# Converting the first layer's weights in a PSUM bank without GpSimd, with a longer landing time for DMAs in the plan

## Chip, cores and metric

The kernel runs on one core of a Trainium2 chip. The metric is the device time of one execution in microseconds (us). TensorE (PE) multiplies, VectorE (DVE), ScalarE (ACT) and GpSimd (POOL) do elementwise work, and SyncE (SP) issues all DMAs. Each engine has a queue of its own and works through it in order.

## What is computed

Linear attention, then two feed-forward stages. The inputs of the first weights are 64-bit floats, which the kernel has to read from their two 32-bit words.

```python
q_s = softmax(q, axis=-1); k_s = softmax(k, axis=2)          # batch 4, heads 8, seq 576, head_dim 64
x = einsum('bhsd,bhde->bhse', q_s, einsum('bhsd,bhse->bhde', k_s, v))   # -> 2304 x 512
h = x @ w_in                                                 # 512 -> 2048, float64 weights
x = (h * clip(h + 3, 0, 6) / 6) @ w_out                      # 2048 -> 512, float64 weights
p = domain_probs / (domain_probs.sum(-1) + 1e-9)
out = sum(p[:, e] * (max(x @ w1[e], 0) @ w2[e]) for e in range(4))      # 512 -> 1024 -> 512
```

## The kernel before

Every product is made of two or three matmuls of a number split in a high part (rounded to the form that PE takes) and a low part (the rest). A split is therefore two steps: ScalarE writes the high part, and VectorE or GpSimd subtracts it from the number.

**Order.** The program first notes all steps in a list (`add`), with the engines that may do each, its cost, the steps it needs, and the buffers that it takes and gives back. `Plan.order` then goes through a model of time: whenever an engine is free, it takes the ready step with the least key, mostly the due time. The order so found is the order of each engine's queue. In that model `LAND` is the time from the end of a DMA's slot on SP until a step that needs its data can start. Only the order comes from the model; on the chip each queue waits on semaphores.

**Attention.** For each of four batches, `k_part` handles four head pairs (key maxima L449, exponential L451, transposes on PE L430, copies L456 and L342 or L344, products with v L437, scaling by reciprocal L444 and L445) and `q_part` five tiles of queries (L494 to L507: maxima, subtract on Pool, exponential, sums, reciprocal, multiply on Pool, transposes L492). `x_part` multiplies both (L531) and splits the result in a high (L534, ScalarE) and a low part (L538, VectorE). They use six PSUM banks `pa` (2 to 7) in the first batch and two (2 and 3) later.

**First layer.** Its work is cut in 96 blocks: a chunk c of 128 hidden columns (of 16) by a block of 384 tokens (of 6). `PASSES1` sets which chunks go with which tokens, three to six chunks at a time. `h_part` makes a block's first product (L638 to L640, 12 matmuls of 384 columns), clips it (L652, ScalarE), gates it (L655, VectorE) and splits it (L661, ScalarE; the low part on Pool or VectorE). `y_part` makes the second product (L682, 12 matmuls). A first product takes a PSUM bank of kind `ph`: banks 0 and 1 during attention, and 2 and 3 as well when attention is done. The gate gives it back.

**Conversion of the weights.** `w_half` turns one half (128 x 512) of a chunk's weights from 64-bit floats into a high and a low part, 32 halves in all. In its order: load L576; o1 (L586, VectorE) takes the exponent out of the upper word into a buffer `wt`; o2 (L590, ScalarE) rebases it; o3 and o3b (L592, L595, VectorE) put in the sign and leave the mantissa's upper part in the raw buffer; o4 (L598, ScalarE) makes a float of it there; o5 (L601, VectorE) adds the lower word; o6 (L605, here L347) multiplies by the power of two; o7 (L606, ScalarE) writes the high part into a weight tile; o8 (L609, here L347) writes the low part. L347 is the line of a helper that records an elementwise operation, on Pool if there is a choice; o6 and o8 are on Pool in all 32 halves. The weight tiles of chunks 6 to 15 come free when the last block of an earlier chunk is done.

**Second stage.** `w_prepare` makes seven forms of the last stage's weights during the first layer (L831 on ScalarE, then Pool), stores them in DRAM (`vd`) and reuses the tile; later units load them again (L864). Three units of 768 tokens follow (L1094 and L1216; then L973 and L1289 twice).

Of the kernel before, what the change touches and what calls it, by code (L numbers as in the profile page):

```python
# [9 lines left out]
F32 = mybir.dt.float32  # L10
F32R = mybir.dt.float32r
I32 = mybir.dt.int32
U32 = mybir.dt.uint32
AF = mybir.ActivationFunctionType
ALU = mybir.AluOpType
# [5 lines left out]
DM = H * D  # L21
# [45 lines left out]
NW, NG, NT_ = 24, 2, 3  # L67
# [4 lines left out]
NX, NXG = 24, 7  # L72
# [4 lines left out]


HOPS = {"PE": 0.06, "ACT": 0.05, "DVE": 0.05, "Pool": 0.09, "SP": 0.05, "": 0.0}
LAND = 1.9  # L80


class Cost(float):
# [9 lines left out]
def hop(a, b):  # L93
    return LAND if a == "SP" else HOPS[b]


def dve(n):
    return Cost(0.064 + n / 960)
# [6 lines left out]
def dve2(n):  # L105
    return Cost(0.064 + n / 960, 0.08, True)


def act(n):
    return Cost(0.092 + n / 1200, 0.1)  # L110


def actp(n):
    return Cost(0.05 + n / 1200, 0.1)


def pool_(n):
    return Cost(0.16 + 2.1e-3 * n if n < 600 else 3.25e-3 * n, 0.05, True)
# [10 lines left out]
def dma(n):  # L129
    return Cost(n / 400.0, 0.0)  # L130
# [21 lines left out]
class Plan:  # L152
# [12 lines left out]
    def add(self, eng, fn, deps=(), take=None, give=(), key=None, due=None):  # L165
        self.ops.append(Op(eng, fn, deps, take, give, key, due))
        return self.ops[-1]
# [100 lines left out]
def tile_kernel(ctx: ExitStack, tc: tile.TileContext, q, kt, v, w64, w, p, out):  # L268


    nc = tc.nc
# [39 lines left out]
    PS = [ps.tile([P, 512], F32, name=f"ps{i}") for i in range(8)]  # L311
# [7 lines left out]
    def on(o):  # L319
        return nc.gpsimd if o.on == "Pool" else nc.vector  # L320

    plan = Plan()
    for kind, n in (("kt", 4), ("ek", 3), ("v", 3), ("q", 5), ("pa", 6), ("raw", 4),
                    ("wt", 4), ("w", NW), ("ph", 2), ("g", NG), ("t", NT_), ("x", NX - 4),
                    ("raw2", 0), ("wtmp", 0), ("xt", 0), ("wr", 0),
                    ("raw0", 0), ("wtmp0", 0), ("y", 0)):
        plan.places(kind, range(n))
    add = plan.add
    in_turn = {}

# [15 lines left out]
    def tt(o, out, a, b, op):  # L346
        on(o).tensor_tensor(out=out, in0=a, in1=b, op=op)  # L347
# [203 lines left out]
    def half_sub(o, out, x, hi):  # L551
        tt(o, out, x, hi.bitcast(F32), ALU.subtract)
# [8 lines left out]
    w0, w_done, w_place = {}, {}, {}  # L561
# [12 lines left out]
    def w_half(c, i, space):  # L574
        early = c < PASSES1[0][1]
        ld = load("raw", {"SP": dma(512)}, lambda o: nc.sync.dma_start(  # L576
            out=RAW[o.place].bitcast(mybir.dt.int64), in_=w64[c, i]), (),
            ("raw", lambda n: n < 2 or early))

        def word(k, dt):  # L580
            return RAW[ld.place].bitcast(dt).rearrange("p (n t) -> p n t", t=2)[:, :, k]

        def t(dt):
            return WT[o1.place].bitcast(dt)

        o1 = add({"DVE": Cost(0.33, 0.08, True)}, lambda o: nc.vector.tensor_scalar(  # L586
            out=WT[o.place].bitcast(I32), in0=word(1, I32), scalar1=20, scalar2=0x7FF,
            op0=ALU.logical_shift_right, op1=ALU.bitwise_and), [ld],
            ("wt", lambda n: n < 2 or early))
        o2 = add({"ACT": Cost(0.61, 0.1)}, lambda o: nc.scalar.activation(  # L590
            out=t(I32), in_=t(I32), func=AF.Relu, scale=2.0**23, bias=rebase), [o1])
        o3 = add({"DVE": dve2(DM)}, lambda o: nc.vector.scalar_tensor_tensor(  # L592
            out=t(I32), in0=word(1, I32), scalar=-(2**31), in1=t(I32),
            op0=ALU.bitwise_and, op1=ALU.bitwise_or), [o2])
        o3 = add({"DVE": Cost(0.33, 0.08, True)}, lambda o: nc.vector.tensor_scalar(  # L595
            out=word(1, I32), in0=word(1, I32), scalar1=0xFFFFF, scalar2=None,
            op0=ALU.bitwise_and), [o3])
        o4 = add({"ACT": act(DM)}, lambda o: nc.scalar.activation(  # L598
            out=word(1, F32), in_=word(1, I32), func=AF.Copy, scale=2.0**-20, bias=1.0),
            [o3])  # L600
        o5 = add({"DVE": dve2(DM)}, lambda o: nc.vector.scalar_tensor_tensor(  # L601
            out=word(1, F32), in0=word(0, U32), scalar=2.0**-52, in1=word(1, F32),
            op0=ALU.mult, op1=ALU.add), [o4])
        o6 = add({"Pool": pool_(DM), "DVE": dve2(DM)}, lambda o: tt(
            o, t(F32), word(1, F32), t(F32), ALU.mult), [o5], None, [("raw", ld)])  # L605
        o7 = add({"ACT": act(DM)}, lambda o: nc.scalar.activation(  # L606
            out=w0[c, i, 0], in_=t(F32), func=AF.Copy), [o6] + space)
        o8 = add({"Pool": pool_(DM), "DVE": dve2(DM)}, lambda o: half_sub(
            o, w0[c, i, 1], t(F32), w0[c, i, 0]), [o7], None, [("wt", o1)])  # L609
        stage_ops.append(o8)  # L610
        return o8

# [789 lines left out]
    for i in range(RING):  # L1402
        o = add(NONE, lambda o: None, ring, ("w", None), (), 0.0)
        o.give.append(("wr", o))
    for i in range(MORE_W + RING):
        o = add(NONE, lambda o: None, stage2, ("wr", None), (), 0.0)
# [6 lines left out]
    for i in range(NXG):  # L1413
        o = load("xg", NONE, lambda o: None, [evicted[NK - 1]], ("x", None), 0.0)
# [120 lines left out]
```

## Time and profile before

| what | value |
|---|---|
| three runs | 1231.95, 1235.85, 1236.56 us; median 1235.85 |
| profiled execution | 1234.68 us, its span 1232.9 us |
| busy share of the span | PE 97%, VectorE 63%, POOL 61%, ScalarE 49% |
| granted clock of PE, mean | 0.994 of full |

The page gives the busy time of each engine, its course in 40 slices, and the chain of work that ended last. PE is busy 5, 6, 9 and 9 tenths in the first four slices of 31 us each, and 9 or more in nearly all others. Of the other views, the windows give busy time by stretch, the timeline gives single instructions with the idle time ahead of each and what ended it, the groups by line and shape give counts and mean durations, and the list of waits says who waited for whom. A step's duration in these rows reaches a little into that of its successor: an undisturbed step of VectorE on 512 columns lasts 0.68 us, and the next one starts 0.60 us after it.

### The profile page before, as it was taken

The page shows a single profiled execution, that of the slowest core. Times are in us where ns is not written, and L with a number is a line of the kernel's source. Part 1 is how long each engine was busy: PE and PEld are TensorE (multiplying, and loading weights), DVE is VectorE, ACT ScalarE, POOL GpSimd, SP SyncE. Part 2 cuts the span into 40 slices and gives each one's busy share as a digit, 9 for nine tenths or more (in the row PEclk, how much of TensorE's full clock was granted, in tenths as well). Part 3 has the DMA queues.
Part 4 walks back from the last instruction along what each step waited for, and adds up shares of the span by engine and source line. Part 5 has one row for each costly group of instructions (what it writes and reads, how often), then busy time and mean ns, then how long its engine had stood idle before and what let it go on. Part 6 is the DMA issues. An engine that isn't in the chain of part 4 may idle for free.

```text
span 1232.9 us, 21178 instructions
## 1 busy us (share of the span) xinstructions
PE 1197.6 (97%) x7296; PEld 1146.5 (93%) x7296; DVE 779.1 (63%) x1362; ACT 600.7 (49%) x1256; POOL 757.7 (61%) x780
## 2 busy tenths in 40 slices
PE   5699999999999999999999999999999999999998
PEld 4589999999999999988988889999999999999998
DVE  6877731668763555555555575666666966666665
ACT  6667544645554543644444444444444544444441
POOL 4677677766688630877777705655555565555552
PEclk9899999999999999999999999999999999999999
DMA  9533444244367430565555547877777787777771
GB/s 318 154 95 104 162 162 164 103 145 147 135 222 256 152 131 1 178 214 180 182 182 190 183 159 232 275 248 250 249 248 250 241 294 250 247 247 249 246 249 59
DMA packets 125275, 238.99 MB, mean 194 GB/s; under 512 B 14064, under 2 KB 14064, under 8 KB 125168
## 3 DMA queue, kind: packets, MB, share of 16 engines
q1 hardware_dynamic: 125168, 237.64, 57.9%
q8 instruction: 58, 0.95, 0.3%
q14 instruction: 49, 0.40, 0.1%
HBM read 174.14 MB, written 63.44 MB: 193 GB/s over the span
## 4 chain that ended last, share of the span: by engine, by line
PE 80%; POOL 6%; DMA 5%; DVE 4%; issue 3%; ACT 1%; SPq 0%; DVEq 0%; POOLq 0%; ACTq 0%
PE ps L1289 19%; PE ps L973 19%; PE ps L1216 11%; PE ps L1094 9%; PE ps L682 9%; POOL w L347 3%; PE ps L638 3%; PE ps L640 3%; PE ps L639 3%; DMA vd<-w 3%; POOL st L347 1%; DMA qs<-in_q_dram 1%; PE ps L437 1%; POOL wtmp L347 1%; PE ps L531 1%
## 5 line engine op out<-in xcount | busy, mean ns | idle before, releaser
L973 PE MATMUL ps<-x,w 128*128 128x384 f32 x1344 | 264.4, 335 | 0.0
L1289 PE MATMUL ps<-w,g 128*128 128x256 f32 x1737 | 244.0, 283 | 1.7 <-DVE acc L1338 1.7
L347 POOL TENSOR_TENSOR w<-st,w 128x256 fp32r<-128x256 f32 (+1 forms) x174 | 173.8, 1016 | 114.7 <-ACT w L931 76.8
L1289 PEld LDWEIGHTS ps<-w,g 128*128 128x128 f32 x1737 | 228.6, 189 | 5.0 <-DVE acc L1338 5.0
L682 PE MATMUL ps<-g,w 128*128 128x384 f32 x1152 | 223.2, 339 | 5.0 <-ACT g L661 4.1
L973 PEld LDWEIGHTS ps<-x,w 128*128 128x128 f32 x1344 | 227.2, 189 | 0.8
L347 POOL TENSOR_TENSOR g<-t,g 128x384 fp32r<-128x384 f32 x128 | 140.9, 1109 | 124.8 <-ACT g L996 108.4
L682 PEld LDWEIGHTS ps<-g,w 128*128 128x128 f32 x1152 | 199.4, 188 | 12.4 <-ACT g L661 7.6
L1338 DVE SCALAR_TENSOR_TENSOR acc<-ps,pt,acc 128x256 f32<-128x256 f32 x312 | 144.2, 480 | 99.2 <-PE ps L1289 97.6
L1216 PE MATMUL ps<-w,g 128*128 128x512 f32 x576 | 148.9, 394 | 0.0
L1094 PE MATMUL ps<-x,w 128*128 128x384 f32 x672 | 131.0, 335 | 0.0
L655 DVE SCALAR_TENSOR_TENSOR r<-r,ps 128x384 f32<-128x384 f32 x96 | 53.0, 552 | 122.1 <-ACT r L652 114.4
L638 PE MATMUL ps<-x,w 128*128 128x384 f32 x384 | 129.0, 336 | 0.0
L640 PE MATMUL ps<-x,w 128*128 128x384 f32 x384 | 128.5, 335 | 0.3 <-POOL w L347 0.3
L639 PE MATMUL ps<-x,w 128*128 128x384 f32 x384 | 128.3, 334 | 0.0
L1094 PEld LDWEIGHTS ps<-x,w 128*128 128x128 f32 x672 | 119.4, 188 | 7.8
L1216 PEld LDWEIGHTS ps<-w,g 128*128 128x128 f32 x576 | 106.6, 188 | 16.7
L347 POOL TENSOR_TENSOR st<-st 128x256 f32<-128x256 f32 (+1 forms) x66 | 74.4, 1131 | 48.6 <-DVE st L601 45.3
L996 ACT ACTIVATE g<-t 128x384 fp32r<-128x384 f32 x143 | 74.6, 525 | 59.3 <-DVE t L1038 21.6
L652 ACT ACTIVATE r<-ps,three 128x384 f32<-128x384 f32 x96 | 55.4, 577 | 76.1 <-PE ps L640 75.0
L347 POOL TENSOR_TENSOR t<-t 128x384 f32<-128x384 f32 x47 | 47.9, 1020 | 45.3 <-ACT t L981 38.9
L981 ACT ACTIVATE t<-ps 128x384 f32<-128x384 f32 x104 | 50.3, 484 | 52.1 <-PE ps L973 51.5
(145 smaller groups left out, 1852.4 us busy)
## 6 DMA issues: line engine op xcount, KB each, us to landing
w<-wd SPq DMA_DIRECT2D x224, 256.0 KB, 3.1
w<-vd SPq DMA_DIRECT2D x224, 256.0 KB, 3.6
vd<-w SPq DMA_DIRECT2D x112, 256.0 KB, 2.2
wd<-w SPq DMA_DIRECT2D x112, 256.0 KB, 3.5
st<-in_w_dram SPq DMA_DIRECT2D x64, 256.0 KB, 3.5
st<-in_w_dram SPq DMA_DIRECT2D x30, 512.0 KB, 3.9
raw<-in_w_dram SPq DMA_DIRECT2D x32, 256.0 KB, 3.7
out_dram<-acc SPq DMA_DIRECT2D x18, 256.0 KB, 2.5
```

The source lines that it names most:

```text
L347: on(o).tensor_tensor(out=out, in0=a, in1=b, op=op)
L638: nc.tensor.matmul(pst[0], lhsT=hi, rhs=a, start=(k == 0), stop=False)
L639: nc.tensor.matmul(pst[0], lhsT=hi, rhs=b, start=False, stop=False)
L640: nc.tensor.matmul(pst[0], lhsT=lo, rhs=a, start=False, stop=(k == NK - 1))
L652: nc.scalar.activation(out=pst["r"], in_=pst[0], func=AF.Relu, bias=three)
L682: nc.tensor.matmul(y, lhsT=l, rhs=r, start=(s["start"] and not low and m == 0), stop=(s["stop"] and bool(low)))
L973: nc.tensor.matmul(bank(i), lhsT=l, rhs=r, start=(opens and k == 0 and m == 0), stop=(k == 1 and m == 2), skip_group_check=not opens)
L996: nc.scalar.activation(out=made[i][0][:, :n], in_=at(src), func=AF.Relu if raw else AF.Copy)
L1094: nc.tensor.matmul(bank(i), lhsT=l, rhs=r, start=(opens and k == 0 and m == 0), stop=(k == 1 and m == 2), skip_group_check=not opens)
L1216: nc.tensor.matmul(y, lhsT=l, rhs=rr, start=opens and x == 0, stop=closes and x == len(seq) - 1)
L1289: nc.tensor.matmul(y, lhsT=l, rhs=r, start=clears and x == 0, stop=x == len(seq) - 1, skip_group_check=True)
L1338: o1 = add({"DVE": dvep(half)}, lambda o: nc.vector.scalar_tensor_tensor(out=a, in0=y, scalar=s, in1=a, op0=ALU.mult, op1=ALU.add), [made])
```

## The change

`w_half` makes steps o4 to o8 in a PSUM bank. ScalarE's o4 writes the float there, VectorE's o5 and o6 work in it in place, ScalarE's o7 reads it for the high part, and VectorE's o8 reads it for the low part. Pool takes part in none of it. The bank is number 1, a buffer kind `pw` with one place; it is taken by o4 and given back by o8. Kind `ph` loses it: one bank (0) during attention and three (0, 2 and 3) afterwards. The raw buffer is given back by o5 instead of o6, and `wt` by o6 instead of o8. The weight tiles (`space`) are now needed by o4 instead of o7. Apart from that `LAND` is 4.0 instead of 1.9, which reorders all queues. Since lines are added, those behind L598 have numbers higher by 2 to 5 in the changed kernel: the first product is L643 to L645 there, the second L687, the clip L657, the gate L660, the high part of a split L666, a weight form L836, o4 L602, o5 L605, o6 L608, o7 L610 and o8 L612; attention's lines are higher by 1.

```diff
-LAND = 1.9
+LAND = 4.0
...
-                    ("wt", 4), ("w", NW), ("ph", 2), ("g", NG), ("t", NT_), ("x", NX - 4),
+                    ("wt", 4), ("w", NW), ("ph", 1), ("g", NG), ("t", NT_), ("x", NX - 4),
...
+    plan.places("pw", [1])
...
+        def f():
+            return PS[o4.place]
+
         o4 = add({"ACT": act(DM)}, lambda o: nc.scalar.activation(
-            out=word(1, F32), in_=word(1, I32), func=AF.Copy, scale=2.0**-20, bias=1.0),
-            [o3])
-        o5 = add({"DVE": dve2(DM)}, lambda o: nc.vector.scalar_tensor_tensor(
-            out=word(1, F32), in0=word(0, U32), scalar=2.0**-52, in1=word(1, F32),
-            op0=ALU.mult, op1=ALU.add), [o4])
-        o6 = add({"Pool": pool_(DM), "DVE": dve2(DM)}, lambda o: tt(
-            o, t(F32), word(1, F32), t(F32), ALU.mult), [o5], None, [("raw", ld)])
-        o7 = add({"ACT": act(DM)}, lambda o: nc.scalar.activation(
-            out=w0[c, i, 0], in_=t(F32), func=AF.Copy), [o6] + space)
-        o8 = add({"Pool": pool_(DM), "DVE": dve2(DM)}, lambda o: half_sub(
-            o, w0[c, i, 1], t(F32), w0[c, i, 0]), [o7], None, [("wt", o1)])
+            out=f(), in_=word(1, I32), func=AF.Copy, scale=2.0**-20, bias=1.0),
+            [o3] + space, ("pw", None))
+        o5 = add({"DVE": dve(DM)}, lambda o: nc.vector.scalar_tensor_tensor(
+            out=f(), in0=word(0, U32), scalar=2.0**-52, in1=f(),
+            op0=ALU.mult, op1=ALU.add), [o4], None, [("raw", ld)])
+        o6 = add({"DVE": dve(DM)}, lambda o: nc.vector.tensor_tensor(
+            out=f(), in0=f(), in1=t(F32), op=ALU.mult), [o5], None, [("wt", o1)])
+        o7 = add({"ACT": actp(DM)}, lambda o: nc.scalar.activation(
+            out=w0[c, i, 0], in_=f(), func=AF.Copy), [o6])
+        o8 = add({"DVE": dve(DM)}, lambda o: nc.vector.tensor_tensor(
+            out=w0[c, i, 1], in0=f(), in1=w0[c, i, 0].bitcast(F32), op=ALU.subtract),
+            [o7], None, [("pw", o4)])
```

The order moves in all queues. Three places follow, of before and of the changed kernel each. The first is VectorE where the low parts of the third token block's x (x0_20 to x0_23) stand, for which PE waits at 61.20 us. Before:

```order
L601 SCALAR_TENSOR_TENSOR acc_81<-acc_81 128x512
L592 SCALAR_TENSOR_TENSOR acc_81<-acc_81 128x512
L592 SCALAR_TENSOR_TENSOR st0_113<-st0_113 128x512
L595 TENSOR_SCALAR acc_81<-acc_81 128x512
L538 TENSOR_TENSOR x0_20_167<-ps3_118,x0_20_167 128x384
L538 TENSOR_TENSOR x0_21_168<-ps2_117,x0_21_168 128x384
L499 TENSOR_REDUCE qm1_105<-qs1_98 128x8
L494 TENSOR_REDUCE qm3_107<-spare2_111 128x8
L494 TENSOR_REDUCE qm4_108<-spare3_112 64x8
L538 TENSOR_TENSOR x0_22_169<-ps3_118,x0_22_169 128x384
L538 TENSOR_TENSOR x0_23_170<-ps2_117,x0_23_170 128x384
```

Here VectorE in the changed kernel (ps1 is the bank of the conversion):

```order
L612 TENSOR_TENSOR w_1_1_1_157<-ps1_116,w_1_1_0_156 128x512
L450 TENSOR_REDUCE nm1_101<-acc_81 128x1
L450 TENSOR_REDUCE nm2_102<-acc_81 128x1
L605 SCALAR_TENSOR_TENSOR ps1_116<-st0_113,ps1_116 128x512
L450 TENSOR_REDUCE nm3_103<-spare0_109 128x1
L539 TENSOR_TENSOR x0_20_166<-ps3_118,x0_20_166 128x384
L608 TENSOR_TENSOR ps1_116<-ps1_116,st0_113 128x512
L539 TENSOR_TENSOR x0_21_167<-ps2_117,x0_21_167 128x384
L495 TENSOR_REDUCE qm2_106<-qs2_99 128x8
L539 TENSOR_TENSOR x0_22_168<-ps3_118,x0_22_168 128x384
L612 TENSOR_TENSOR w_2_0_1_159<-ps1_116,w_2_0_0_158 128x512
L539 TENSOR_TENSOR x0_23_169<-ps2_117,x0_23_169 128x384
```

Before, four steps of three halves stand ahead of the x steps; now the last four steps of conversions ahead of and among them (o8 of w_1_1, then o5, o6 and o8 of w_2_0) all work in bank 1.

The second place is PE behind the first product of block 0 with chunk 0 (its last matmul, L640 or L645, is the first row). Before, up to the transposes of the next keys:

```order
L640 MATMUL ps0_115<-x0_03_152,w_0_0_1_148 128x384
L492 MATMUL ps3_118<-ident_87,qs0_97 128x128 x4
L492 MATMUL ps2_117<-ident_87,qs1_98 128x128 x4
L531 MATMUL ps3_118<-qt_86,bd2_91 128x192
L531 MATMUL ps2_117<-qt_86,bd0_89 128x192
L437 MATMUL ps3_118<-vs0_95,acc_81 128x129 x5
L531 MATMUL ps2_117<-qt_86,bd3_92 128x192
L531 MATMUL ps3_118<-qt_86,bd2_91 128x192
L437 MATMUL ps2_117<-vs1_96,acc_81 128x129 x5
L531 MATMUL ps3_118<-qt_86,bd1_90 128x192
L531 MATMUL ps2_117<-qt_86,bd3_92 128x192
L492 MATMUL ps3_118<-ident_87,qs2_99 128x128 x4
```

In the changed kernel, up to the second product of the same block:

```order
L645 MATMUL ps0_115<-x0_03_151,w_0_0_1_147 128x384
L532 MATMUL ps2_117<-qt_86,bd3_92 128x192
L438 MATMUL ps3_118<-vs1_96,acc_81 128x129 x5
L532 MATMUL ps2_117<-qt_86,bd0_89 128x192
L532 MATMUL ps3_118<-qt_86,bd3_92 128x192
L532 MATMUL ps2_117<-qt_86,bd1_90 128x192
L532 MATMUL ps3_118<-qt_86,bd2_91 128x192
L431 MATMUL ps2_117<-ident_87,acc_81 128x128 x4
L431 MATMUL ps3_118<-ident_87,acc_81 64x128
L687 MATMUL ps4_119<-g_503,w_0_1_0_152 128x384
```

Before, the second product stands behind fourteen rows of attention work, in the changed kernel behind eight; the first product with chunk 1 follows it there at once, where before nine more rows of attention work stand among and behind the second product's rows.

The third place is ScalarE in the first layer's later passes, near the conversion of chunk 11. Rows L831 or L836 write the forms of the last stage's weights (w_7_5_1 is form 5 of pair 7); a conversion writes w_11_0_0. Before:

```order
L831 ACTIVATE w_7_7_1_2777<-wtmp_2608 128x256
L652 ACTIVATE r_2820<-ps0_115,three_84 128x384
L831 ACTIVATE w_7_5_1_2828<-wtmp_2661 128x256
L661 ACTIVATE g_2834<-r_2820 128x384
L598 ACTIVATE st0_113<-st0_113 128x512
L590 ACTIVATE st1_114<-st1_114,rebase_85 128x512
L831 ACTIVATE w_7_6_1_2860<-wtmp_2685 128x256
L652 ACTIVATE r_2864<-ps1_116,three_84 128x384
L661 ACTIVATE g_2875<-r_2864 128x384
L606 ACTIVATE w_11_0_0_2416<-st0_113 128x512
```

Now:

```order
L602 ACTIVATE ps1_116<-st0_113 128x512
L836 ACTIVATE w_6_7_1_2815<-wtmp_2617 128x256
L657 ACTIVATE r_2819<-ps3_118,three_84 128x384
L610 ACTIVATE w_11_0_0_2359<-ps1_116 128x512
L836 ACTIVATE w_6_5_1_2828<-wtmp_2636 128x256
L666 ACTIVATE g_2837<-r_2819 128x384
L602 ACTIVATE ps1_116<-st1_114 128x512
```

Beside the same conversion stand forms of pair 7 before and of pair 6 now.

## Rows read from the trace of the kernel before

**Rows 1.** The page: span, and busy time of PE (share, instructions).

```profile
span 1232.9 us, 21178 instructions
PE 1197.6 (97%) x7296; PEld 1146.5 (93%) x7296; DVE 779.1 (63%) x1362; ACT 600.7 (49%) x1256; POOL 757.7 (61%) x780
```

**Rows 2.** Windows: length, PE, PEld, DVE, ACT, POOL busy, granted clock, DMA share, GB/s.

```profile
41.98:71.50 29.52, 21.77 (x112) 16.18 (x111) 25.41 (x54) 19.50 (x44) 17.62 (x15) 0.88 0.40 119
71.50:106.80 35.30, 33.79 (x218) 30.75 (x219) 26.74 (x59) 25.56 (x56) 24.29 (x21) 1.00 0.36 113
...
30.00:40.00 10.00, 7.62 (x38) 6.72 (x39) 7.68 (x21) 4.62 (x13) 7.56 (x7) 0.67 0.59 186
60.00:70.00 10.00, 8.80 (x38) 7.15 (x39) 8.01 (x19) 4.32 (x10) 6.83 (x7) 0.66 0.19 46
```

**Rows 3.** Timeline of PE, attention: start, length, line; in brackets idle time and releaser.

```profile
31.29 1.30 PE L430 MATMUL ps<-ident,acc 128*128 128x128 f32 x5 [2.98 <-DVE bd L445]
...
61.20 2.93 PE L531 MATMUL ps<-qt,bd 128*128 128x384 f32 x4 [3.32 <-DVE x L538]
```

**Rows 4.** Timeline of VectorE: gates 1, 2 and 8, and two equal steps.

```profile
41.44 0.54 DVE L655 SCALAR_TENSOR_TENSOR r<-r,ps 128x384 f32<-128x384 f32 x1
...
57.12 0.68 DVE L592 SCALAR_TENSOR_TENSOR acc<-acc 128x512 int32<-128x512 int32 x1
57.72 1.78 DVE L592 SCALAR_TENSOR_TENSOR st<-st 128x512 int32<-128x512 int32 x1
...
71.28 0.55 DVE L655 SCALAR_TENSOR_TENSOR r<-r,ps 128x384 f32<-128x384 f32 x1 [0.47 <-ACT r L652]
...
106.29 0.56 DVE L655 SCALAR_TENSOR_TENSOR r<-r,ps 128x384 f32<-128x384 f32 x1 [0.36 <-ACT r L652]
```

**Rows 5.** Groups, 41.98 to 106.8 us (mean ns); then by line (least/median/most ns).

```profile
L601 DVE SCALAR_TENSOR_TENSOR st<-st 128x512 f32<-128x512 uint32 x5 | 4.7, 934 | 0.0
L592 DVE SCALAR_TENSOR_TENSOR st<-st 128x512 int32<-128x512 int32 x5 | 4.6, 921 | 1.2 <-ACT st L590 1.2
L595 DVE TENSOR_SCALAR st<-st 128x512 int32<-128x512 int32 x6 | 3.6, 603 | 0.0
...
L601 DVE SCALAR_TENSOR_TENSOR st<-st x30: 679/686/1774, 29.4 to 419.8; 128x512 f32<-128x512 uint32 x30
L592 DVE SCALAR_TENSOR_TENSOR st<-st x30: 636/689/1814, 20.8 to 417.4; 128x512 int32<-128x512 int32 x30
L595 DVE TENSOR_SCALAR st<-st x30: 372/421/1424, 21.7 to 418.5; 128x512 int32<-128x512 int32 x30
```

**Rows 6.** Helper line L347: least/median/most ns; last row, o6 in 0 to 110 us.

```profile
L347 DVE TENSOR_TENSOR t<-ps,t x79: 541/558/559, 506.1 to 1211.9; 128x384 f32<-128x384 f32 x79
L347 DVE TENSOR_TENSOR g<-r,g x69: 544/560/1629, 128.3 to 497.9; 128x384 fp32r<-128x384 f32 x69
L347 DVE TENSOR_TENSOR t<-t x26: 546/560/1116, 504.0 to 1166.5; 128x384 f32<-128x384 f32 x26
...
L347 POOL TENSOR_TENSOR st<-st 128x512 f32<-128x512 f32 x7 | 10.1, 1439 | 7.4 <-DVE st L601 7.4
```

**Rows 7.** Waits (total us, times, longest), then timeline rows of ACT, PE and POOL.

```profile
ACT w L831 <- DMA vd<-w: 43.0, 45, 4.1
PE ps L682 <- ACT g L661: 4.1, 7, 1.5
...
290.97 0.42 ACT L831 ACTIVATE w<-wtmp 128x256 fp32r<-128x256 f32 x1 [4.13 <-DMA vd<-w]
291.85 2.35 PE L682 MATMUL ps<-g,w 128*128 128x384 f32 x12 [1.47 <-ACT g L661]
494.31 2.53 POOL L347 TENSOR_TENSOR w<-st,w 128x512 fp32r<-128x512 f32 x2 [51.19 <-ACT w L931]
```

**Rows 8.** DMA issues: count, KB each, median us from issue to landing.

```profile
acc<-in_kt_dram SPq DMA_DIRECT2D x13, 288.0 KB, 3.5
st<-in_w_dram SPq DMA_DIRECT2D x30, 512.0 KB, 3.9
```

## The prediction, made before the changed kernel ran

> **What bounds the kernel now.** I read the page's head and busy times first [rows 1]: TensorE is busy 97% of the span, so a change elsewhere counts only where PE stands still or runs slowly. The windows place this: PE is busy 21.8 of the 29.5 us up to 71.5 us, and 33.8 of the 35.3 behind [rows 2]; after 90 us nearly all of the rest is a few stalls of the first layer's later passes, 4.1 us in seven waits of PE's second products for a split made by ScalarE [rows 7]. So two places can move the end: the attention stage up to about 107 us, and the stretch from 240 to 420 us. Behind them the queues of PE, ScalarE, VectorE and SP hold the same kinds of operation in the same order before and after, and PE never waits for a load there; I cost this part at nothing. What hides it is a full PE; if its loads came late they would show as PE waits on w<-wd.
>
> In the attention stage PE waits for VectorE: at 31.29 us for the scaling of a head pair, at 61.20 us for a low part of x [rows 3]. VectorE's queue shows why [rows 4]: 57.12 and 57.72 us are the same operation of two weight halves, 0.60 us apart when undisturbed, and the second took 1.78. Between the first gate (41.44 us) and the second (71.28 us) VectorE is busy 25.4 of 29.5 us, 86%; from there to the eighth gate (106.29 us) 26.7 of 35.3, 76%, since PE is then the limit [rows 2, 4]. A gate is the VectorE step L655 of a first-layer block, and counts blocks.
>
> **The change, part by part.** *Conversion.* Each of 32 halves moves two Pool operations (o6 and o8; 1.44 us for o6 in the first 110 us [rows 6]) to VectorE, as operations with an operand in PSUM. No row shows VectorE reading and writing one PSUM bank; the bounds are 0.60 us, the start-to-start time of a 512-wide step [rows 4], and 0.93, the mean of such a step under Pool's disturbance [rows 5]. I take 0.60, since steps with a PSUM operand show no disturbance: 541/558/559 ns (least, median, most), against 1629 ns at most for one with all operands in SBUF [rows 6].
>
> [...]
>
> *What VectorE has to do up to the eighth gate.* By then the changed order has as many first products on PE as before, 36 more second-product matmuls (some 6 us) and less attention work of about the same 6 us (three kv groups, ten transposes of k, four 192-wide x products): PE's task up to this gate is equal. VectorE's between gates 1 and 8 is not. Added: 16 operations o6 and o8 (9.6 us), two more o5 and one more o3 (1.8), two key maxima, two evictions and the four steps on the shares that stood ahead of gate 1 before (3.4). Gone: four reciprocal and scaling pairs, two sums, five 192-wide low parts, one o1 (4.9). Sum: 9.9 us more.
>
> Against that stands relief. In this stretch 16 of the port-sharing steps run 934, 921 and 603 ns on average where their medians are 686, 689 and 421: (0.248 x 5) + (0.232 x 5) + (0.182 x 6) = 3.5 us, 0.22 each [rows 5]. There are 29 such steps of four lines before, 6.4 us, and 22 after. Pool's 41.9 us of work in the two windows [rows 2] falls by 14 operations of about 1.4 us to half; I estimate 22 x 0.11 = 2.4 us. Relief: 4.0 us.
>
> So VectorE has 52.1 + 9.9 - 4.0 = 58.0 us to do where it had 52.1 in 64.8. If it is now the limit all the way and keeps the 86% of the first window, that takes 58.0 / 0.861 = 67.4 us, **2.6 us more**. PE cannot win lost time back, since it is full behind. The share is the unknown: 93% gives 62.4 us (-2.4), the second window's 76% gives 76.6 us (+11.8). I take 86%, the row of the stretch in which VectorE is the limit now.
>
> *One bank instead of two for first products (ph), one for the conversion (pw).* With one ph bank a first product waits for the gate of the last. In the changed PE order a second product (12 matmuls, 2.35 us with the last one's tail [rows 7]) or attention work stands between them nearly everywhere; the gate, 0.54 us [rows 4], and a clip of like length on ScalarE come after the product, so this hides unless VectorE's queue is late, which the share above covers. After attention three banks are left of four, with two such products, some 4.2 us, per block: nothing. The PSUM bank is held from o4 to o8, five steps that alternate between ScalarE and VectorE, some 3 us at least if ScalarE's two steps are as long as VectorE's three.
>
> *Space.* o4 now waits for the weight tiles, where only o7 did. Behind o4 on ScalarE stand clips and splits of the main work. This matters once, where chunks 6 to 8 take the tiles of chunks 0 to 2: six halves in about six blocks of 4.2 us. At 4 us each it is just enough; PE would lose under 1 us.
>
> *LAND.* Loads of keys and weights take 3.5 and 3.9 us [rows 8], not 1.9: the plan now counts 4.0. In the first layer's later passes ScalarE stood 43.0 us in 45 waits for a weight form's tile that a store still read; one of them, 4.13 us up to 290.97, delayed the split behind it and so PE at 291.85 by 1.47 [rows 7]. The changed order has these forms some seven places later beside the same conversion. It can return up to the 4.1 us of PE's waits. But VectorE has more there too, since 20 of the halves are converted in it (24 us more) while Pool has less. Ends: -4.1 and +3; I take -1. Pool's forms end about three blocks later; its pause of 51.19 us behind them covers this [rows 7].
>
> **Sum.** Start +2.6, later passes -1, the rest 0: +1.6 us. The profiled execution was 1234.68 us around a span of 1232.9, 1.2 us under the median of 1235.85; its sum is 1236.3, and moved to the median it is **1237.5**.
>
> **Rivals.** *VectorE and ScalarE wait for each other (slower).* A half now hands over four times between two queues that each run in order; Pool, which took two of the five steps, let VectorE go on. In the changed VectorE queue o5, o6 and o8 stand between the x steps on which PE waits; a late o7 on ScalarE stops them all. If the busy share falls to the second window's 76%, the stage is 11.8 us longer and no gain is left later: 1247.7. It decides slower from a share of 81% (58.0 / 0.81 = 71.6, +6.8). For it: two hand-overs more per half, and VectorE's 58 us there are 8 us per block where PE needs some 4.2 and the attention work. Against: ScalarE's own load does not grow. 0.31.
>
> *The order fits the chip (faster).* [...] 0.26.
>
> *The bank is too slow at the turn of the tiles.* At 5.5 us per half the six halves take 8 us more than six blocks: 1244. Part of the slower chance (0.04 of it).
>
> *The change does nothing*, because the attention stage is paced by its loads and buffers: 1235.9, within the forecast's case.
>
> **How the numbers follow.** Forecast 0.43 (own range 1231 to 1243), slower rivals 0.31, faster rival 0.26. No change that a measurement here can tell is within 0.5%, 6.2 us: 1229.7 to 1242.0. The range reaches to both sides' rivals and leaves out about one in ten at each end: 1226 to 1249. Faster 0.26, same 0.43, slower 0.31.
>
> **What would show it.** Right: gate 8 at 107 to 111 us, VectorE busy 85% or more from gate 1 to gate 8, Pool under 25 us there, the port-sharing steps near their medians. Slower rival: idle time of VectorE ahead of o5, o6 and o8, put down to ScalarE. Faster rival: gate 8 before 104 us, no window of low clock, no ScalarE wait for vd<-w over 2 us. Wrong altogether: PE waits behind 500 us, or steps on PSUM of 0.75 us and more.

## The result, and the profile after

The changed kernel took **1213.26 us** (median of four runs, 1212.97 to 1213.55), against 1235.54 for the kernel before: a ratio of 0.9825, 95% interval [0.9805, 0.9845]. That is 22 us less. The prediction was 1237.5 with a range of 1226 to 1249, so it was wrong: next to no change was forecast, and the range ends 13 us above the time.

The head of the page after (span, busy times, the shares of the chain that ended last) stands against [rows 1]:

```profile
span 1210.9 us, 21155 instructions
PE 1190.0 (98%) x7296; PEld 1145.9 (95%) x7296; DVE 790.3 (65%) x1426; ACT 593.0 (49%) x1255; POOL 665.6 (55%) x717
PE 92%; DVE 5%; ACT 1%; issue 0%; POOL 0%; DMA 0%; DVEq 0%; ACTq 0%; POOLq 0%
```

One pair of numbers holds the whole result. The weight loads of PE (PEld) are 7296 in both, and busy 1146.5 us before and 1145.9 after. So the time in which PE loaded no weights is 1232.9 - 1146.5 = 86.4 us before and 1210.9 - 1145.9 = 65.0 after: 21.4 us less, of 22.0 us of span. The matmul row shows two thirds of it: 1232.9 - 1197.6 = 35.3 us not busy before, 20.9 after.

Where it went is read from the gates. The timeline of VectorE after (start, length, line; idle time and releaser in brackets), gates 1, 2, 8, 15, 36 and 78, against [rows 4]:

```profile
38.84 0.55 DVE L660 SCALAR_TENSOR_TENSOR r<-r,ps 128x384 f32<-128x384 f32 x1 [0.32 <-ACT r L657]
52.34 0.54 DVE L660 SCALAR_TENSOR_TENSOR r<-r,ps 128x384 f32<-128x384 f32 x1
94.67 0.54 DVE L660 SCALAR_TENSOR_TENSOR r<-r,ps 128x384 f32<-128x384 f32 x1
137.88 0.55 DVE L660 SCALAR_TENSOR_TENSOR r<-r,ps 128x384 f32<-128x384 f32 x1 [2.46 <-ACT r L657]
225.31 0.56 DVE L660 SCALAR_TENSOR_TENSOR r<-r,ps 128x384 f32<-128x384 f32 x1 [0.40 <-ACT r L657]
400.63 0.55 DVE L660 SCALAR_TENSOR_TENSOR r<-r,ps 128x384 f32<-128x384 f32 x1 [0.83 <-ACT r L657]
```

Gates 15, 36 and 78 of the kernel before, in the same view:

```profile
149.11 0.56 DVE L655 SCALAR_TENSOR_TENSOR r<-r,ps 128x384 f32<-128x384 f32 x1 [1.24 <-ACT r L652]
236.47 0.56 DVE L655 SCALAR_TENSOR_TENSOR r<-r,ps 128x384 f32<-128x384 f32 x1 [3.60 <-ACT r L652]
421.81 0.56 DVE L655 SCALAR_TENSOR_TENSOR r<-r,ps 128x384 f32<-128x384 f32 x1 [1.37 <-ACT r L652]
```

With gate 15 attention is over in both. By then 11.2 us are gained. From gate 15 to 36 both take 87.4 us, from 36 to 78 the changed kernel takes 175.3 instead of 185.3 (10.0 us), and behind gate 78 the two differ by 0.8 us. So there are two gains: 11 us in the attention stage and 10 us in the later passes of the first layer.

The windows of both kernels say what each gain is made of (length; busy time of PE, PEld, DVE, ACT, POOL; granted clock; DMA share; GB/s). Before, up to gate 15 and from gate 36 to 78:

```profile
0.00:149.11 149.11, 125.08 (x725) 109.30 (x726) 113.89 (x242) 99.69 (x215) 95.97 (x92) 0.95 0.51 165
236.47:421.81 185.34, 179.95 (x1010) 173.71 (x1009) 119.66 (x193) 97.97 (x204) 135.97 (x146) 1.00 0.51 174
```

After, up to gate 15, from gate 1 to past the eighth, between gates 15 and 36, and from gate 36 to 78:

```profile
0.00:137.88 137.88, 122.02 (x725) 107.77 (x726) 116.16 (x264) 95.54 (x209) 56.94 (x64) 0.99 0.52 173
38.84:95.23 56.39, 52.87 (x305) 45.46 (x303) 55.60 (x124) 43.08 (x95) 25.01 (x25) 0.97 0.42 136
137.88:225.31 87.43, 87.43 (x507) 87.43 (x506) 29.46 (x52) 38.10 (x83) 48.54 (x60) 1.00 0.35 121
225.31:400.63 175.32, 175.32 (x1009) 174.56 (x1009) 125.66 (x222) 97.98 (x214) 100.36 (x128) 1.00 0.58 198
```

Up to gate 15 PE does the same task, 726 weight loads in both. They are busy 109.30 us before and 107.77 after, 1.5 us less at a granted clock of 0.99 instead of 0.95; and PE stands without a weight load for 39.8 us before and 30.1 after, 9.7 less. In the later passes the weight loads stand still for 11.6 us before and 0.8 after. 21 blocks with full weight loads take 87.4 us, so 42 take 174.8: the changed kernel is at that pace, and the kernel before lost 10.5 us against it.

What the weight loads waited for from 225 to 420 us (total us, times, longest), before:

```profile
PEld ps L682 <- ACT g L661: 7.6, 11, 1.8
PEld ps L682 <- DVE g L347: 1.6, 4, 0.7
PEld ps L682 <- DVE acc L724: 0.7, 4, 0.2
PEld ps L640 <- POOL w L347: 0.7, 1, 0.7
PEld ps L682 <- issue: 0.6, 1, 0.6
```

And after:

```profile
PEld ps L687 <- ACT g L666: 0.6, 2, 0.3
PEld ps L645 <- DVE w L612: 0.2, 1, 0.2
```

11.2 us in 21 waits before, mostly for the split that ScalarE writes, and 0.8 after. ScalarE's own waits for vd<-w, of which [rows 7] shows 43.0 us in the whole run, 33.2 of them from 225 to 420 us, are gone there: no row of that kind is left for ScalarE. The two hang together. Each wait of the weight loads can be followed back in the trace, from what ended it to what that step had waited for itself. Of the 21 waits before, 15 (8.3 of the 11.2 us) lead back so to a wait of ScalarE for a store, some directly, some by way of VectorE or Pool; after, none does.

### The profile page after: what moved, and what is told of

It reads as the page before. It is cut to its first block, busy times and chain, and to the rows that moved or that the text cites. A ratio compares the mean times of both kernels' runs of the same rounds, so it can differ in the third digit from the quotient of the medians.

```text
span 1210.9 us, 21155 instructions
## 1 busy us (share of the span) xinstructions
PE 1190.0 (98%) x7296; PEld 1145.9 (95%) x7296; DVE 790.3 (65%) x1426; ACT 593.0 (49%) x1255; POOL 665.6 (55%) x717
## 4 chain that ended last, share of the span: by engine, by line
PE 92%; DVE 5%; ACT 1%; issue 0%; POOL 0%; DMA 0%; DVEq 0%; ACTq 0%; POOLq 0%
PE ps L1294 19%; PE ps L978 18%; PE ps L687 16%; PE ps L1221 11%; PE ps L1099 10%; PE ps L645 5%; PE ps L643 5%; PE ps L644 5%; PE ps L438 1%; PE ps L532 1%; PE ps L431 1%; DVE acc L1343 1%; DVE x L348 0%; DVE x L539 0%; PE ps L493 0%
## 5 line engine op out<-in xcount | busy, mean ns | idle before, releaser
L978 PEld LDWEIGHTS ps<-x,w 128*128 128x128 f32 x1344 | 227.2, 189 | 0.8
L687 PE MATMUL ps<-g,w 128*128 128x384 f32 x1152 | 223.2, 339 | 1.6 <-ACT w L610 1.2
L348 POOL TENSOR_TENSOR g<-t,g 128x384 fp32r<-128x384 f32 x131 | 144.4, 1113 | 126.5 <-ACT g L1001 111.2
L687 PEld LDWEIGHTS ps<-g,w 128*128 128x128 f32 x1152 | 201.8, 189 | 4.4 <-ACT w L610 1.4
L348 POOL TENSOR_TENSOR w<-st,w 128x256 fp32r<-128x256 f32 (+1 forms) x144 | 133.0, 944 | 106.1 <-ACT w L936 66.6
L660 DVE SCALAR_TENSOR_TENSOR r<-r,ps 128x384 f32<-128x384 f32 x96 | 53.0, 552 | 118.0 <-ACT r L657 114.9
L643 PE MATMUL ps<-x,w 128*128 128x384 f32 x384 | 129.0, 336 | 0.0
L645 PE MATMUL ps<-x,w 128*128 128x384 f32 x384 | 128.6, 335 | 0.3 <-DVE w L612 0.3
L1099 PEld LDWEIGHTS ps<-x,w 128*128 128x128 f32 x672 | 119.4, 188 | 7.8
L657 ACT ACTIVATE r<-ps,three 128x384 f32<-128x384 f32 x96 | 55.7, 581 | 138.6 <-PE ps L645 138.2
L1001 ACT ACTIVATE g<-t 128x384 fp32r<-128x384 f32 x160 | 82.8, 524 | 80.0 <-DVE t L1065 36.7
L348 POOL TENSOR_TENSOR w<-wtmp,w 128x256 fp32r<-128x256 f32 x64 | 49.7, 779 | 50.8 <-ACT w L836 50.7
L645 PEld LDWEIGHTS ps<-x,w 128*128 128x128 f32 x384 | 72.1, 188 | 0.8 <-DVE w L612 0.8
L643 PEld LDWEIGHTS ps<-x,w 128*128 128x128 f32 x384 | 72.1, 188 | 0.2
```

What stands on the lines that cost most here:

```text
L643: nc.tensor.matmul(pst[0], lhsT=hi, rhs=a, start=(k == 0), stop=False)
L645: nc.tensor.matmul(pst[0], lhsT=lo, rhs=a, start=False, stop=(k == NK - 1))
L657: nc.scalar.activation(out=pst["r"], in_=pst[0], func=AF.Relu, bias=three)
L687: nc.tensor.matmul(y, lhsT=l, rhs=r, start=(s["start"] and not low and m == 0), stop=(s["stop"] and bool(low)))
L978: nc.tensor.matmul(bank(i), lhsT=l, rhs=r, start=(opens and k == 0 and m == 0), stop=(k == 1 and m == 2), skip_group_check=not opens)
L1001: nc.scalar.activation(out=made[i][0][:, :n], in_=at(src), func=AF.Relu if raw else AF.Copy)
```

## The experiments

Two parts of the change can be set apart at once: the number `LAND`, and the conversion in PSUM. The table holds what all runs gave; the reading of each stands below it. "Busy" and "still" are the weight loads' time up to gate 15 and the rest of the time up to it (the task is equal: 726 weight loads by that gate in all, but 720 in dve_extra; the busy time goes with the granted clock, from 105.5 us at 1.00 in dve_sbuf to 110.0 at 0.95 in land_only). The last two columns are gate 36 to 78, and the sum of the weight loads' waits from 225 to 420 us. The gates are those of one traced execution of each kernel. Each ratio is to runs of the kernel before made beside that kernel; their median was 1233.1 us for free_4, load_4, pool_junk and dve_extra and 1235.5 to 1235.7 for the others, so small differences between medians of the two groups mean little.

| kernel | median us | ratio to before | gate 15 | busy | still | 36 to 78 | waits |
|---|---|---|---|---|---|---|---|
| before | 1235.5 | | 149.1 | 109.3 | 39.8 | 185.3 | 11.2 |
| changed | 1213.3 | 0.9825 [0.9805, 0.9845] | 137.9 | 107.8 | 30.1 | 175.3 | 0.8 |
| land_only | 1223.2 | 0.9907 [0.9885, 0.9928] | 147.0 | 110.0 | 37.0 | 176.3 | 1.6 |
| psum_only | 1228.1 | 0.9944 [0.9927, 0.9960] | 140.6 | 106.3 | 34.3 | 183.6 | 10.9 |
| dve_sbuf | 1218.2 | 0.9866 [0.9849, 0.9884] | 140.6 | 105.5 | 35.2 | 177.3 | 2.0 |
| pool_junk | 1220.0 | 0.9892 [0.9874, 0.9910] | 141.1 | 107.5 | 33.7 | 178.0 | 3.5 |
| free_4 | 1222.6 | 0.9908 [0.9892, 0.9924] | 141.6 | 108.9 | 32.7 | 179.2 | 4.7 |
| load_4 | 1222.8 | 0.9907 [0.9889, 0.9926] | 138.3 | 108.9 | 29.4 | 184.8 | 12.3 |
| one_bank | 1230.0 | 0.9958 [0.9946, 0.9971] | 149.9 | 109.1 | 40.8 | 177.8 | 3.3 |
| space_late | 1212.5 | 0.9815 [0.9801, 0.9830] | 136.9 | 105.9 | 31.0 | 175.1 | 0 |
| dve_extra | 1222.5 | 0.9908 [0.9892, 0.9924] | 141.1 | 106.5 | 34.6 | 179.6 | 5.0 |
| shares_late | 1214.4 | 0.9832 [0.9817, 0.9847] | 138.1 | 105.9 | 32.2 | 175.4 | 0.8 |
| land3 | 1218.6 | 0.9864 [0.9849, 0.9878] | 144.1 | 109.5 | 34.6 | 174.9 | 0.2 |
| land6 | 1220.6 | 0.9882 [0.9865, 0.9898] | 140.9 | 108.9 | 32.0 | 177.1 | 2.6 |

In twelve of these fourteen kernels the last two columns agree within 1 us when 174.8 is taken from the first of them (185.3 - 174.8 = 10.5 beside 11.2), and in the other two (psum_only and load_4) within 2.4; there 1003 and 999 weight loads lie between the two gates, in the others 1007 to 1011. So the weight loads' waits are the loss.

**One half of the change each.** The kernel before with the longer landing time:

```diff
-LAND = 1.9
+LAND = 4.0
```

> The kernel before with the landing time at 4.0 alone; the conversion stays with Pool in SBUF. Theory 1 (the attention stage gains 11 us by the conversion in PSUM, the later passes 10 us by the landing time): about 1225 us, gate 15 near 149 us as before, gates 36 to 78 in some 175 us instead of 185. Theory 2 (the landing time, and so the order, gives both): 1213 to 1216 us, gate 15 near 138 us. Theory 3 (the conversion gives both): 1233 to 1237 us.

The changed kernel with the old one:

```diff
-LAND = 4.0
+LAND = 1.9
```

> The changed kernel with the landing time back at 1.9. Theory 1: about 1224 us, gate 15 at 138 to 140 us, gates 36 to 78 in some 185 us. Theory 2: 1233 us or more, gate 15 at 149 us or later, since VectorE has more to do and the order is the old one in kind. Theory 3: 1213 to 1216 us.

The landing time alone gives 12.3 us, 9.0 of them in gates 36 to 78 and 2.1 by gate 15. The conversion alone gives 7.4: 8.5 by gate 15, and nothing from there to gate 78, which takes 272.8 us against 272.7 before. 12.3 and 7.4 make 19.7 of the 22: the two gains have different causes in the main. The later passes are the landing time's, as ScalarE's waits from 225 to 420 us show. land_only:

```profile
ACT w L831 <- DMA vd<-w: 1.4, 1, 1.4
```

psum_only:

```profile
ACT w L836 <- DMA vd<-w: 25.9, 28, 2.7
```

With 1.9 in the plan ScalarE still comes 28 times to a tile that a store still reads; with 4.0, on the old conversion, once. The stores themselves say why. A store of 256 KB has a slot of 0.64 us in the plan, so with 1.9 behind it the tile counts as free after 2.5 us, and with 4.0 after 4.6. Of the 74 stores of the kernel before that were issued from 225 to 420 us, 35 took longer than 2.5 us to land and two longer than 4.6; the median was 2.3, the longest 5.7, and that one is behind the wait of 4.13 us in [rows 7].

**Which DMAs the landing time is about.** In the model it counts twice: for a step that needs a load's data, and for a buffer that a DMA has to give back. Each run takes 4.0 for one of them and 1.9 for the other:

```diff
 def hop(a, b):
-    return LAND if a == "SP" else HOPS[b]
+    return (LAND if b else FREE) if a == "SP" else HOPS[b]
```

In free_4 the 4.0 stands for the buffer, in load_4 for the data.

> The changed kernel with the landing time split: 4.0 only where a DMA frees a buffer, 1.9 where a step waits for a load's data. If the later passes are cured because forms no longer stand on ScalarE ahead of the stores that free their tiles: gates 36 to 78 in 175 to 177 us, ScalarE waits for vd<-w under 3 us in 225 to 420 us, and about 1214 to 1218 us. If it is the loads' time: 183 us or more for these gates and 1221 us or more.

> The other half: 4.0 where a step waits for a load's data, 1.9 where a DMA frees a buffer. If the release counts: gates 36 to 78 in 182 us or more, ScalarE waits for vd<-w of 20 us or more, about 1221 to 1226 us. If the loads count: 1213 to 1217 us.

From 225 to 420 us, ScalarE's waits for stores and those of the weight loads, in free_4 (4.0 for what a DMA gives back):

```profile
ACT w L837 <- DMA vd<-w: 0.4, 1, 0.4
PEld ps L688 <- ACT g L667: 2.3, 3, 1.1
PEld ps L688 <- DVE g L349: 1.9, 2, 1.3
```

In load_4 (4.0 for what a load brings):

```profile
ACT w L837 <- DMA vd<-w: 28.8, 20, 3.9
PEld ps L688 <- ACT g L667: 8.0, 8, 2.0
PEld ps L688 <- DVE g L349: 2.8, 6, 0.9
```

So ScalarE's waits for stores end with the release half. In load_4 all 22 waits of the weight loads lead back to a store, in free_4 none. The release half gives 4.4 us of the later passes (183.6 to 179.2), less than was expected of it (175 to 177 us), the load half alone none (184.8). Both together give 175.3, but what the load half adds there is not shown: the six other kernels that count 4.0 for both stand between 175.1 and 179.6, and free_4's 179.2 lies within. Up to gate 15 PE stands still for 29.4 us in load_4 and 30.1 in the changed kernel, against 32.7 and 34.3 where loads count 1.9; that points to the load half, but differences of this size come with any new order (below). Loads of keys and weights landed 4.3 and 4.0 us after their issue in the changed kernel (medians).

**VectorE instead of Pool, or the bank?** dve_sbuf is land_only with o6 and o8 on VectorE alone, still in SBUF, with two banks for first products:

```diff
-        o6 = add({"Pool": pool_(DM), "DVE": dve2(DM)}, lambda o: tt(
+        o6 = add({"DVE": dve2(DM)}, lambda o: tt(
...
-        o8 = add({"Pool": pool_(DM), "DVE": dve2(DM)}, lambda o: half_sub(
+        o8 = add({"DVE": dve2(DM)}, lambda o: half_sub(
```

> The kernel before with the landing time at 4.0, and o6 and o8 on VectorE alone, but still in SBUF with two ph banks. If taking Pool out is what counts: 1213 to 1216 us. [...]

pool_junk is the changed kernel with two products on Pool per half that nothing uses:

```diff
+        for d in (o5, o7):
+            add({"Pool": pool_(DM)}, lambda o: nc.gpsimd.tensor_tensor(
+                out=junk, in0=junk, in1=junk, op=ALU.mult), [d])
```

> The changed kernel with two more Pool products of 128x512 per weight half, on a scratch tile that nobody needs: Pool is as busy as before, and nothing waits for it but Pool's own queue. [...] If what counted was that the conversion no longer waits in Pool's queue: gate 15 within 2 us of the changed kernel's 137.9.

The groups of VectorE by shape say what happens to its steps (count, busy us, mean ns, idle before). After, gate 1 to past the eighth, the steps of the conversion, against [rows 5]:

```profile
L612 DVE TENSOR_TENSOR w<-ps,w 128x512 fp32r<-128x512 f32 x8 | 5.4, 680 | 0.0
L608 DVE TENSOR_TENSOR ps<-ps,st 128x512 f32<-128x512 f32 x7 | 4.8, 686 | 0.0
L605 DVE SCALAR_TENSOR_TENSOR ps<-st,ps 128x512 f32<-128x512 uint32 x7 | 4.8, 680 | 0.0
L593 DVE SCALAR_TENSOR_TENSOR st<-st 128x512 int32<-128x512 int32 x6 | 4.1, 682 | 0.0
L587 DVE TENSOR_SCALAR st<-st 128x512 int32<-128x512 int32 x6 | 2.5, 410 | 0.0
```

dve_sbuf, 45.6 to 101.5 us, o3, o6 and o8 in SBUF:

```profile
L592 DVE SCALAR_TENSOR_TENSOR st<-st 128x512 int32<-128x512 int32 x6 | 5.7, 946 | 0.0
L347 DVE TENSOR_TENSOR st<-st 128x512 f32<-128x512 f32 x5 | 5.0, 991 | 0.0
L347 DVE TENSOR_TENSOR w<-st,w 128x512 fp32r<-128x512 f32 x5 | 3.4, 681 | 0.0
```

pool_junk, 36.1 to 101.9 us: o3, o8, o1 and o6:

```profile
L594 DVE SCALAR_TENSOR_TENSOR st<-st 128x512 int32<-128x512 int32 x7 | 5.7, 821 | 0.1
L613 DVE TENSOR_TENSOR w<-ps,w 128x512 fp32r<-128x512 f32 x8 | 5.4, 677 | 0.4 <-ACT w L611 0.4
L588 DVE TENSOR_SCALAR st<-st 128x512 int32<-128x512 int32 x6 | 4.1, 692 | 0.0
L609 DVE TENSOR_TENSOR ps<-ps,st 128x512 f32<-128x512 f32 x6 | 4.1, 683 | 0.0
```

A step with both operands in SBUF can be stretched when Pool has more work (946 and 991 ns in dve_sbuf, with Pool busy 29.8 of 55.9 us; 821 in pool_junk, 46.2 of 65.8; 682 after, 25.0 of 56.4), though not each one is (o8 in dve_sbuf took 681). A step on PSUM is not (means of 677 to 686 in both): in each of the ten kernels that convert in the bank, the slowest of the 96 steps there took at most 700 ns, while the slowest two-input step of that width in SBUF took 1221 to 1814 ns, by kernel, in all fourteen. So the change relieves VectorE twice: Pool has less to do, and three of VectorE's six steps per half are out of its reach. The time that PE stands still up to gate 15 goes from 37.0 us (land_only) over 35.2 (o6 and o8 on VectorE, in SBUF) to 30.1 (in PSUM), and with Pool's load put back it is 33.7. These differences are near what an order's luck is worth (below), so their sum, 6.9 us, is better known than their parts, and how much of it is the bank's is not shown. o1, with one input, goes from 410 ns in the changed kernel to 692 in pool_junk; why, no row tells.

**What the prediction costed at nothing.** one_bank is the kernel before with one bank for first products in place of two:

```diff
-                    ("wt", 4), ("w", NW), ("ph", 2), ("g", NG), ("t", NT_), ("x", NX - 4),
+                    ("wt", 4), ("w", NW), ("ph", 1), ("g", NG), ("t", NT_), ("x", NX - 4),
```

> The kernel before with one bank less for first products (ph has place 0 alone until attention is done, and bank 1 stays unused) and nothing else. If the lost bank costs nothing, as the prediction had it: 1234 to 1237 us. If a first product has to wait for the gate of the last one: 1240 us or more, with PE waits for L655 in the attention stage.

space_late lets o7 wait for the weight tiles again, and not o4:

```diff
-            [o3] + space, ("pw", None))
+            [o3], ("pw", None))
...
-            out=w0[c, i, 0], in_=f(), func=AF.Copy), [o6])
+            out=w0[c, i, 0], in_=f(), func=AF.Copy), [o6] + space)
```

> The changed kernel, but the weight tiles are needed by o7 again and not by o4, so that a half waiting for its tiles holds the PSUM bank. If o4's early need of the tiles costs nothing (the prediction): within 2 us of 1213. If holding it back matters at the turn of the tiles (gates 33 to 40): up to 4 us faster; if the bank then stands idle but taken: slower by as much.

The bank costs 0.8 us by gate 15 and the early space under 1 us (1212.53 against 1213.26, intervals that overlap): both were rightly costed. But one_bank fits neither of its two cases: it gained 7.5 us in gates 36 to 78, with the old landing time and the old conversion, which one bank less up to gate 15 does not explain by itself, since later passes have three. Its waits from 225 to 420 us, of ScalarE for stores and of the weight loads:

```profile
ACT w L831 <- DMA vd<-w: 20.1, 24, 3.0
PEld ps L682 <- ACT g L661: 1.9, 3, 1.0
```

ScalarE still waits 20.1 us for stores (24 waits; before 33.2 us in 31), yet the waits of the weight loads that lead back to a store are 2.3 us here and 8.3 before. So a wait for a store costs something only where work that PE needs soon stands behind it, and the order decides that. What in this order keeps them apart was not found. It also means that an order can cure most of the later passes' loss without the landing time: of the four kernels that count 1.9 for a store three take 183.6 us or more there, and one_bank 177.8.

**Is VectorE the limit of the attention stage?** dve_extra puts one more step of 0.6 us on VectorE ahead of every o6, which nothing uses; shares_late takes four steps on the shares out of the stage.

```diff
+            nc.vector.tensor_reduce(out=peak, in_=junk, axis=AX.X, op=ALU.max)
             nc.vector.tensor_tensor(out=f(), in0=f(), in1=t(F32), op=ALU.mult)
```

> The changed kernel with one more VectorE step (a maximum over 512 columns of a scratch tile, 0.6 us) ahead of each o6. If VectorE is the limit of the attention stage after the change, as its busy share of 98% from 40 to 90 us says: gate 15 later by 5 to 8 us (12 halves at 0.6 us), 1219 to 1224 us. If its queue is only full of waits that the trace counts as busy: under 2 us.

```diff
-        norm.append(add({"DVE": Cost(1.0)}, normal, [ld]))
+        norm.append(add({"DVE": Cost(1.0)}, normal, [ld], None, [], None, 90.0))
```

> The changed kernel with the four VectorE steps on the shares (1.8 us in all) given a late due time, out of the stretch from 38 to 95 us in which VectorE is never idle. If VectorE's work there sets the pace: 1 to 2 us faster than the changed kernel, 1211 to 1212 us. If not: 1213 to 1215 us.

The 12 halves that are converted by gate 15 get 12 x 0.6 = 7.2 us more work; gate 15 comes 3.2 us later, with six weight loads (1.0 us) still to do that the changed kernel had behind it. That is less than the 5 to 8 us expected if VectorE were the limit all the way, and more than the 2 us of the other case. 1.8 us less work gives nothing (138.1 against 137.9). So VectorE's work seems to count at a part of its length, as if it were the limit in parts of the stage only; but 3 to 4 us are also what an order's luck is worth (below), and so this is not shown. dve_extra also lost 4.3 us in gates 36 to 78, which 20 halves of 0.6 us there do not explain by their length while PE is the limit; the weight loads' waits grew from 0.8 to 5.0 us.

**Is 4.0 special?** The changed kernel with 3.0 and with 6.0:

```diff
-LAND = 4.0
+LAND = 3.0
```

> The changed kernel with the landing time at 3.0, under the median landing of loads (3.5 to 4.0 us) and over that of the stores (2.3). If what counts is that the plan's time is not under the real one: later than 1213 by 2 to 8 us, in part by the start (load waits), with gates 36 to 78 at 176 to 180 us. If any other order than that for 1.9 does: 1213 to 1216 us.

```diff
-LAND = 4.0
+LAND = 6.0
```

> The changed kernel with the landing time at 6.0, over every median landing. If a plan that waits longer than the chip costs nothing but some idle buffers: 1211 to 1217 us, gates 36 to 78 at 175 to 177 us. If it delays loads and forms too far: 1218 us or more, with PE waits at the turn of the tiles.

Neither run fits its cases well: land3 is slower as expected, but not in gates 36 to 78, and land6 loses 3.1 us behind gate 78, away from the turn of the tiles. Any of 3.0, 4.0 and 6.0 removes most of the later passes' loss (174.9, 175.3, 177.1). At gate 15 they stand at 144.1, 137.9 and 140.9: neither monotone nor explained by landing. So an order's own luck is worth some 3 to 6 us there, of which up to 1.7 is the clock (busy 107.8 to 109.5) and the rest stalls. Part of the 11 us by gate 15 may be such luck. No kernel was found that is faster than the changed one beyond its interval.

## Why the prediction was wrong, point by point

**The step that failed first: VectorE's busy share.** The prediction read 86% from [rows 2], took the rest as a property of the stage, and divided the new work by it. Measured, VectorE is busy 55.60 of 56.39 us from gate 1 to past gate 8, 98.6%, above the 93% that was the upper end, and gate 8 follows gate 1 in 55.8 us where 67.4 were predicted and 64.9 stood before. Its waits in that stretch of the kernel before (41.44 to 106.85 us, total us, times, longest) show what its idle time there was, 12.7 of 65.4 us:

```profile
DVE r L655 <- ACT r L652: 3.1, 5, 1.0
DVE rs L444 <- PE ps L437: 2.4, 5, 1.0
DVE x L538 <- ACT x L534: 2.2, 4, 0.7
DVE st L592 <- ACT st L590: 1.2, 2, 1.0
```

They are short waits for a result that PE or ScalarE would have soon; after, one wait of 0.3 us is left in the stretch. The runs show that the share goes with who does o6 and o8. From gate 1 to gate 8 (windows as above), psum_only, land_only and, to past gate 8, dve_sbuf:

```profile
38.60:92.39 53.79, 50.08 (x289) 43.42 (x289) 52.07 (x114) 40.91 (x88) 21.11 (x21) 0.97 0.48 149
45.52:114.23 68.71, 62.41 (x382) 53.97 (x381) 56.77 (x123) 49.05 (x108) 49.95 (x42) 0.95 0.39 117
45.60:101.50 55.90, 51.02 (x306) 43.87 (x307) 54.74 (x115) 42.98 (x94) 29.83 (x26) 1.00 0.41 122
```

VectorE is 80 to 83% busy in the three kernels that leave o6 and o8 to Pool (before, land_only, one_bank) and 95 to 99% in the eleven that have them on VectorE, with the old landing time (psum_only, 97%) as with the new, and in SBUF (dve_sbuf, 98%) as on PSUM. So the idle time was room that steps of VectorE's own could fill, not a tax on them. How they fill it is a reading, not shown: with more work of its own VectorE comes later to the same steps and finds their inputs done. The slower rival, which had the share fall, took the same error further: VectorE and ScalarE hand over four times per half, and no idle time of VectorE ahead of o5, o6 and o8 came up in that stretch.

**The work itself was nearly right.** 58.0 us were expected in the stretch, some 55 were there. Relief was underrated: o3 went to 682 ns, o1 to 410 and o3b to 408, under their medians before (689 and 421 in [rows 5] for o3 and o3b, 428 for o1), where only half of their stretch was counted as gone. The prediction counts them as port-sharing, after a mark `port` that the plan puts on some steps of VectorE and Pool. No run shows that the two share a port; what the rows show is the stretch, of o3 from 682 ns to 821 when Pool's load is put back (pool_junk). Pool's work fell to 25.0 us, about as expected. Steps on PSUM took 680 to 686 ns, like the undisturbed step of [rows 4], and the 0.93 us did not come up. At 98.6% the 58.0 us would have taken 58.8, so of the 11.6 us between 67.4 and 55.8 the share accounts for 8.6 and the work for 3.0.

**The step that failed second: the later passes were bounded by the matmul row.** "It can return up to the 4.1 us of PE's waits" rests on the wait row of [rows 7], and 10.0 came back. A matmul's record lasts 0.33 us while the next matmul starts 0.17 after it, so the matmul row hides a part of every stall: the one of 1.8 us in the weight-load row is 1.47 in [rows 7], and the changed kernel's three of 0.21 to 0.31 us are not there at all (PE busy 175.32 of 175.32 us). That row has 185.3 - 180.0 = 5.4 us of idle time in gates 36 to 78, and the weight-load row, with records of 0.19 us, 11.6. The bound was too small by a factor of 2.4. The +3 set against it, for VectorE's added work, did not come up either: VectorE is busy 125.7 of 175.3 us there, and the weight loads wait 0.2 us for it. The table's last two columns say the same: in all fourteen kernels these gates take 174.8 us and the weight loads' waits, within 2.4 us. The weight-load row was on the page of before: PEld 1146.5 of 1232.9 us [rows 1]. Nor was PE the limit in the second window of [rows 2], as the prediction has it: its weight loads are busy 30.75 of 35.30 us there.

**The faster rival had the places and the way, but not the cause at the start, and was too small.** Its three items, 9.5 us in all, were -2.4 for VectorE at 93% (measured by gate 15: 9.7 us less standing still), -4.1 later (10.0) and -3 for the clock (1.5), an estimate from the 0.67 and 0.66 of [rows 2]. It put the first down to queues that no longer stop for late keys and queries, so to the landing time. The runs have it the other way: with the landing time alone gate 15 comes 2.1 us earlier and VectorE stays at 83%, with the conversion alone 8.5 us earlier at 97%. For the later passes it had the landing time right, but the half that counts there is the stores', not the loads'. Two of its signs came: gate 8 at 94.67 us, before 104; no ScalarE wait for vd<-w from 225 to 420 us. The third, no window of low clock, came in part. The lowest of the twelve 10 us windows from 10 to 130 us in the changed kernel, to be read beside the two of 0.67 and 0.66 in [rows 2]:

```profile
40.00:50.00 10.00, 7.53 (x30) 5.41 (x30) 9.71 (x21) 6.17 (x17) 1.00 (x1) 0.83 0.39 115
```

All in all the clock is the smaller part of the gain.

**Not foreseen at all:** gate 1 comes 2.6 us earlier (38.84 against 41.44). The wait of 2.98 us of [rows 3], for the scaling of a head pair, is 0.65 us or less in the new order, and the granted clock from 20 to 38.84 us is 1.00 (0.82 before).

**Right:** PE's task up to the eighth gate is equal within 2 us (weight loads busy 68.6 and 68.1 us, 482 and 471 of them); one bank for first products and the early space cost under 1 us each; nothing is lost behind 500 us; steps on PSUM are not disturbed by Pool (at most 700 ns, in pool_junk too); Pool's later forms stay hidden.

**What stays open:** how the 9.7 us of stalls up to gate 15 split between the landing time, Pool's lighter load, the bank and the luck of an order, finer than some 3 to 6 us; whether VectorE is the limit of the stage now; and why one_bank has so few stalls in the later passes.

## What to carry to other kernels

Judge what a full PE still loses by its weight-load row, or by the pace from block to block against an undisturbed stretch, and not by the idle time of the matmul row: here the two stood at 11.6 and 5.4 us. Do not carry an engine's busy share over to a changed load; look at what its waits are for, and ask whether those would be over if it came later. Where a plan fixes the order of in-order queues, a latency that it underrates (a store that gives back a buffer as much as a load) puts a wait ahead of work that others need (ScalarE's waits for stores from 225 to 420 us: 25.9 us in psum_only, none in the changed kernel), and correcting it is worth an experiment of its own; but a change of the order alone moves some microseconds either way (3 to 6 by gate 15 here), so vary the number before believing a small part of the gain.

## What the runs showed of the hardware

VectorE reading and writing one PSUM bank in place, on 512 columns, takes 680 to 686 ns on average, the same as an undisturbed step in SBUF (682), and stays there while Pool works (at most 700 ns), where two-input SBUF steps go to 821 to 991 on average in some stretches (pool_junk, dve_sbuf). The next step starts 0.60 us behind it, as behind one in SBUF; after, o3 in SBUF, o8 from the bank, and o3b:

```profile
81.84 0.68 DVE L593 SCALAR_TENSOR_TENSOR st<-st 128x512 int32<-128x512 int32 x1
82.44 0.68 DVE L612 TENSOR_TENSOR w<-ps,w 128x512 fp32r<-128x512 f32 x1
83.04 0.43 DVE L596 TENSOR_SCALAR st<-st 128x512 int32<-128x512 int32 x1
```
